# Splitting q, k and v on ScalarE and VectorE instead of GpSimd, and pacing attention by phase

## Chip, core and metric

One core of a Trainium2 chip runs the program. The metric is its time on the device in microseconds (us), the median of several runs of the same program.

## What is computed

Attention with a sigmoid in place of the softmax, over 8 batches of 12 heads, 448 positions and 64 values a head, feeds an MLP with a piecewise activation. In the reference (cut):

```
scores = scale * np.matmul(q, k.transpose(0, 1, 3, 2)) - np.log(S)     # scale = 1/8, S = 448
attn = 1.0 / (1.0 + np.exp(-scores))
x = np.matmul(attn, v)            # then (8*448, 768): 12 heads side by side
h = x @ w_in                      # w_in 768 x 2048
g = np.where(h >= 1, h, np.where(h <= -1, 0.0, (h + 1) ** 2 / 4))
out = g @ w_out                   # w_out 2048 x 768
```

## The kernel before

All large products run in 16 bit. To keep more digits, a 32-bit operand is scaled and **split**: a high part, the value rounded to 16 bit, and a low part, the remainder; a product of two split operands is three products, high by high, high by low and low by high.

*Attention.* The unit is a pair p of heads, six pairs a batch, 48 in all. Pairs 0 to 7 are used in full 32 bit, pairs 8 to 13 have q and k split, and pairs from 14 on have q, k and v split. `prep_a` (L323) finds the sums of the absolute values of a pair, `prep_b` (L344) turns them into scales, on VectorE, and splits (L365 to L375). Up to pair 16 the split is one ScalarE instruction for the high part (L368) and one VectorE instruction for the low part (L369), for each of q, k and v. From pair 17 (QA = 17) GpSimd does it with three instructions for each: scale in place (L373), round (L374), subtract (L375). A pair goes through four pieces of 128, 128, 128 and 64 keys. `scores` (L410) forms a piece's scores in PSUM (L438), `weigh` (L462) takes the sigmoid on ScalarE (L474) and splits it, high part on ScalarE (L482), low part on VectorE (L483), and `av` (L490) multiplies by v (L520). The last piece of a pair uses a block-diagonal copy of k's last 64 positions, the **corner**, two copies a pair (L454; on VectorE for pairs under CORN = 10, otherwise on GpSimd, and only pairs from 14 on have one).

*MLP.* For batches 0 and 1 the first products (L748, `up`) run plainly over 16 chunks of 128 hidden units. Beside batch 1's products the first weights are mixed (`mix`, L648, on VectorE and ScalarE; buffers pass through DMAs to HBM and back) for a scheme with seven block products instead of eight. From batch 2 on `up_blocks` (L699) does seven products of nine matmuls for each of eight block pairs; VectorE and ScalarE add the quarters up (L723, L726, L732) and `bend` (L755) applies the activation, five instructions for each of 16 chunks: L761 and L764 on ScalarE, L762, L763 and L765 on VectorE. `down` (L769) then does the second products, 288 matmuls a batch (L784). At the end of a batch `start_blocks` and `finish_blocks` (L549, L555) find the maximum of the next x through a product with a diagonal matrix (L163, L173), take four differences of blocks of x (L563 to L566, two on GpSimd by TP = 1) and split seven blocks of x (L569, L570).

*Order.* While batch b is multiplied, attention of batch b + 1 is worked in between, 24 steps a batch. The list `units` of product units is walked, and a table `share` (L933) says how many of the 24 steps are due by each unit: every unit counts DW = 8, but in batch 1 the first 24 units count 4, half. From batch 2 on there are 56 units of first products and 48 of second ones, with all steps due by unit 92. On top of that a scheduler arranges each engine's instructions by priority and its own estimates, so a change in one place can reorder an engine's whole queue. Each engine then works its queue strictly in turn, and waits where an operand is not there.

Of the kernel before, what the change touches and what calls it, by code (L numbers as in the profile page):

```python
# [19 lines left out]
ALU = mybir.AluOpType  # L20
# [30 lines left out]
LSTEP = 3  # L51

SB = 2
QA = 17
QT = 3
CORN = 10
GROUPED = 14
RUN_PRIO = 600
TP = 1

DW = 8
MIX0 = 24
# [9 lines left out]
def sigmoid_attention_mlp(ctx: ExitStack, tc: tile.TileContext, first_qvk, qkv, w_in, w_out, out_t):  # L72
# [271 lines left out]
    def prep_b(p):  # L344
        if not NFULL <= p < NPAIR or not first_time("split", p):
            return
        r, m = raws.pop(p), maxes.pop(p)
        n = 2 if p < NFULL + NHALF else 3
        m = sums.pop(p) if p in sums else all_sum(m, n)

        s, inv = scales(m, n, "qkv")
        sqk = sml_p.tile([P, 2], F32, tag="sqk", name="sqk")
        if n == 3:
            nc.vector.tensor_scalar(out=sqk[:, 1:2], in0=inv[:, 2:3], scalar1=1.0 / ATT, scalar2=None, op0=ALU.mult)
        nc.vector.tensor_scalar(
            out=sqk[:, 0:1], in0=inv[:, 0:1], scalar1=inv[:, 1:2], scalar2=1.0 / math.sqrt(D), op0=ALU.mult, op1=ALU.mult
        )
        hl = hls.pop(p, None) or stk_p.tile([P, 2, 2, S], F16, tag="hl", name="hl")
        parts = [hl[:, 0], hl[:, 1]]
        if n == 3:  # L360
            v = stk_p.tile([P, 2, VW], F16, tag="v", name="v", bufs=3)
            parts.append(v)
        else:
            v = ready[p]
        for t, dst in enumerate(parts):  # L365
            rt, hi = r[:, t * S : 2 * S + VW if t == 2 else (t + 1) * S], dst[:, 0, :]
            if p < QA and t != QT:
                nc.scalar.activation(hi, rt, AF.Copy, scale=s[:, t : t + 1])  # L368
                nc.vector.scalar_tensor_tensor(  # L369
                    out=dst[:, 1, :], in0=rt, scalar=s[:, t : t + 1], in1=hi, op0=ALU.mult, op1=ALU.subtract  # L370
                )
                continue
            nc.gpsimd.tensor_scalar(out=rt, in0=rt, scalar1=s[:, t : t + 1], scalar2=1.0, op0=ALU.mult, op1=ALU.mult)  # L373
            nc.gpsimd.tensor_scalar(out=hi, in0=rt, scalar1=1.0, scalar2=1.0, op0=ALU.mult, op1=ALU.mult)  # L374
            nc.gpsimd.tensor_tensor(out=dst[:, 1, :], in0=rt, in1=hi, op=ALU.subtract)  # L375

        ready[p] = hl, v, sqk

    pieces = {}
# [30 lines left out]
    def scores(todo):  # L410
# [37 lines left out]
        for p, c in (divmod(i, NPC) for i in todo):  # L448
            if c == 0 and p >= NFULL + NHALF:
                if p < NFULL + NHALF + 2:  # L450
                    nc.gpsimd.memset(corner(p), 0.0)
                for j in range(2):
                    rows = slice(j * D, (j + 1) * D)
                    (nc.vector if p < CORN else nc.gpsimd).tensor_copy(  # L454
                        out=corner(p)[rows, :, rows], in_=ready[p][0][rows, 1, :, NKC * P :]
                    )

# [97 lines left out]
    def finish_blocks(xm1, diag):  # L555
# [5 lines left out]
        b11, b12, b21, b22 = (x4[:, r, :, j, :] for r in range(2) for j in range(2))  # L561
        t1, t2, t3, t4 = (rows[:, k * HC * HN : (k + 1) * HC * HN].rearrange("p (c n) -> p c n", c=HC) for k in range(4))
        nc.vector.tensor_tensor(out=t1, in0=b12, in1=b11, op=ALU.subtract)  # L563
        (nc.gpsimd if TP else nc.vector).tensor_tensor(out=t3, in0=b22, in1=b12, op=ALU.subtract)
        nc.vector.tensor_tensor(out=t2, in0=b22, in1=t1, op=ALU.subtract)
        (nc.gpsimd if TP else nc.vector).tensor_tensor(out=t4, in0=b21, in1=t2, op=ALU.subtract)  # L566
        for t, src in ((0, b11), (4, t2), (5, t3), (3, t1), (1, b21), (6, t4), (2, b22)):
            hi = xc[:, t, :, 0, :]
            nc.scalar.activation(hi, src, AF.Copy, scale=s)  # L569
# [354 lines left out]
    for b in range(1, B):  # L924
# [5 lines left out]
            last = len(units) - LAST1  # L930
        first = at

        share = [DW // 2 if b < SB and u < NA * NCC // 2 else DW for u in range(last)]  # L933
        share = [sum(share[:u]) / sum(share) for u in range(last + 1)]
        with ExitStack() as order:
            if b >= PM:
# [63 lines left out]
```

## Time and profile before

| | |
|---|---|
| timed runs, median (lowest to highest) | 1156.87 us (1155.78 to 1158.25) |
| the profiled execution, its own time | 1152.84 us |
| its span, first to last instruction | 1151.1 us |
| TensorE (PE) busy | 1120.0 us, 97% |
| VectorE (DVE) busy | 831.4 us, 72% |
| ScalarE (ACT) busy | 721.2 us, 63% |
| GpSimd (POOL) busy | 291.3 us, 25% |
| mean granted TensorE clock | 0.998 of full |

The profile is one execution on the chip. The matrix engine is PE, and PEld its loading of weights, which runs beside it. An engine's busy time over the whole span says little here, since the stages differ; the same numbers by stretch, the list of what TensorE waited for, and the instructions just ahead of a wait say more. A row of grouped instructions ends with the idle time just before them and what ended it.

### The profile page before, as it was taken

The numbers are of one execution on the slowest core, as the hardware profiler recorded it, in microseconds if no ns is written. First come the engines' busy times: TensorE is split into PE (matmuls) and PEld (weight loads), VectorE is DVE, ScalarE is ACT, GpSimd is POOL, SyncE is SP. The second block draws the span as 40 slices with busy tenths as digits, with TensorE's granted clock in tenths as the row PEclk, the third lists the DMA queues.
The fourth block names the chain that finished last, engine by engine and source line by source line (L and its number), as shares of the span: only waits on it lengthen the run. The fifth ranks groups of instructions, "written<-read, shape, count | busy, mean of one in ns | idle before, by whom it ended". The sixth has DMA issues, their size and how long they took to land.

```text
span 1151.1 us, 20032 instructions
## 1 busy us (share of the span) xinstructions
PE 1120.0 (97%) x7914; PEld 660.7 (57%) x7914; DVE 831.4 (72%) x1730; ACT 721.2 (63%) x1199; POOL 291.3 (25%) x367
## 2 busy tenths in 40 slices
PE   8899999999889999999999999999999998999998
PEld 2234434444446775478645776457754677548954
DVE  6988977789985996469945798368974599646820
ACT  6978988679765785457754687347773476423410
POOL 0000000003442344323623353515344234110000
PEclk9999999999999999999999999999999999999999
DMA  9933432153453653125421345114532054103300
GB/s 367 394 107 132 162 124 74 35 192 119 161 182 120 220 193 108 49 91 193 157 105 50 130 170 195 50 50 169 186 140 69 22 189 173 65 17 123 136 24 25
DMA packets 32511, 151.64 MB, mean 132 GB/s; under 512 B 3488, under 2 KB 14240, under 8 KB 26272
## 3 DMA queue, kind: packets, MB, share of 16 engines
q1 hardware_dynamic: 30688, 140.92, 33.8%
q10 hardware_dynamic: 1728, 9.44, 2.2%
q8 instruction: 62, 1.02, 0.4%
q14 instruction: 33, 0.27, 0.1%
HBM read 126.94 MB, written 23.40 MB: 131 GB/s over the span
## 4 chain that ended last, share of the span: by engine, by line
PE 67%; DVE 20%; ACT 7%; issue 2%; DMA 2%; SPq 0%; DVEq 0%; ACTq 0%
PE po L784 35%; PE ph L714 11%; PE ph L748 8%; PE pav L520 6%; DVE ahl L483 5%; PE psc L438 4%; DVE g L762 4%; DVE g L763 3%; DVE xhl L723 2%; ACT ahl L482 2%; ACT psc L474 2%; DVE ghl L765 1%; PE psc L429 1%; DMA blocks<-mixs 1%; ACT ghl L764 1%
## 5 line engine op out<-in xcount | busy, mean ns | idle before, releaser
L784 PE MATMUL po<-ghl,w_out_sb 128*128 128x448 f16 x2304 | 447.7, 354 | 2.9 <-DVE g L763 2.9
L784 PEld LDWEIGHTS <-w_out_sb 128*128 128x128 f16 x2304 | 222.5, 98 | 220.4 <-issue 19.5
L714 PE MATMUL ph<-w_in_sb 128*128 128x224 f16 x3024 | 303.7, 259 | 10.6 <-DVE xhl L723 10.5
L714 PEld LDWEIGHTS <-w_in_sb 128*128 128x128 f16 x3024 | 284.4, 98 | 37.7 <-issue 36.4
L483 DVE SCALAR_TENSOR_TENSOR ahl<-psc,ahl 128x896 f16<-128x896 f32 (+1 forms) x170 | 153.0, 900 | 113.2 <-ACT ahl L482 111.4
L474 ACT ACTIVATE psc<-psc,nls,sqk 128x896 f32<-128x896 f32 (+1 forms) x136 | 130.3, 971 | 116.6 <-PE psc L438 113.4
L373 POOL TENSOR_SCALAR raw<-raw,qkv_s 128x448 f32<-128x448 f32 (+1 forms) x93 | 68.6, 752 | 427.6 <-DVE qkv_i L137 368.5
L482 ACT ACTIVATE ahl<-psc 128x896 f16<-128x896 f32 (+1 forms) x170 | 128.0, 762 | 23.3 <-DVE ahl L483 21.8
L748 PE MATMUL ph<-xhl,w_in_sb 128*128 128x448 f16 x576 | 112.8, 353 | 0.0
L761 ACT ACTIVATE g<-xhl,hr,ihr 128x448 f32<-128x448 f32 x96 | 67.8, 753 | 56.4 <-DVE xhl L723 56.2
L764 ACT ACTIVATE ghl<-g 128x448 f16<-128x448 f32 x128 | 73.2, 572 | 46.5 <-DVE g L763 46.4
L765 DVE TENSOR_TENSOR ghl<-g,ghl 128x448 f16<-128x448 f32 x128 | 91.1, 718 | 11.9 <-ACT ghl L764 11.0
L723 DVE TENSOR_TENSOR xhl<-ph,xhl 128x224 f32<-128x224 f32 x240 | 86.3, 382 | 16.9 <-PE ph L714 10.6
L762 DVE SCALAR_TENSOR_TENSOR g<-g,rk 128x448 f32<-128x448 f32 x112 | 83.9, 764 | 14.8 <-ACT g L761 14.3
L438 PE MATMUL psc<-hl 64*128 64x448 f16 x756 | 91.3, 352 | 0.3 <-ACT a L471 0.3
L748 PEld LDWEIGHTS <-w_in_sb 128*128 128x128 f16 x576 | 54.6, 98 | 59.9 <-issue 9.7
L520 PE MATMUL pav<-ahl,v 128*64 128x448 f16 x748 | 83.7, 357 | 0.0
L375 POOL TENSOR_TENSOR hl<-raw,hl 128x448 f16<-128x448 f32 x62 | 72.5, 1190 | 0.0
L797 DVE TENSOR_SCALAR o<-po,od 128x448 f32<-128x448 f32 x42 | 28.5, 679 | 59.0 <-PE po L784 58.8
L763 DVE SCALAR_TENSOR_TENSOR g<-xhl,ihs,g 128x448 f32<-128x448 f32 x96 | 69.3, 739 | 0.1
L337 ACT ACTIVATE dump<-raw 128x448 f16<-128x448 f32 (+1 forms) x105 | 61.5, 586 | 2.7 <-DVE mb L154 1.3
L454 POOL COPY w_in_sb<-hl 64x128 f16<-64x128 f16 x68 | 27.8, 409 | 129.3 <-DVE hl L369 127.4
(149 smaller groups left out, 1080.0 us busy)
## 6 DMA issues: line engine op xcount, KB each, us to landing
w_in_sb<-blocks SPq DMA_DIRECT2D x48, 1344.0 KB, 6.0
raw<-qkv SPq DMA_DIRECT2D x34, 704.0 KB, 4.2
w_out_sb<-w_in SPq DMA_DIRECT2D x16, 768.0 KB, 11.1
out_t<-o SPq DMA_DIRECT2D x48, 224.0 KB, 1.9
blocks<-mixs SPq DMA_DIRECT2D x8, 768.0 KB, 3.3
w_out_sb<-w_out ACTq DMA_DIRECT2D x6, 768.0 KB, 4.9
raww<-w_out ACTq DMA_DIRECT2D x6, 768.0 KB, 5.3
blocks<-mixp SPq DMA_DIRECT2D x8, 576.0 KB, 3.4
```

The lines of the kernel that those rows point to most:

```text
L438: run(lambda: nc.tensor.matmul(out, hl[rows, 1, kh, w], hl[rows, 0, qh, :], start=t == 0, stop=t == 2))
L474: nc.scalar.activation(a, a, AF.Sigmoid, bias=nls, scale=sqk)
L482: nc.scalar.activation(hi, x, AF.Copy, scale=ATT)
L483: made.setdefault(i, []).append(nc.vector.scalar_tensor_tensor(out=lo, in0=x, scalar=ATT, in1=hi, op0=ALU.mult, op1=ALU.subtract))
L520: run(lambda: once(nc.tensor.matmul(pav[j * D : (j + 1) * D, :S], *terms[j][t], start=c == 0 and t == 0, stop=mid and t == len(terms[j]) - ...
L714: nc.tensor.matmul(out, w[:, wt, wh, c * P : (c + 1) * P], xc[:, xt, c, xh, :], start=j in (0, 2) and c + wh + xh == 0, stop=c == HC - 1 a ...
L723: add = lambda out, q, other: nc.vector.tensor_tensor(out=out, in0=quarter(q), in1=other, op=ALU.add)
L748: nc.tensor.matmul(ph[:, :S], w_in_sb[:, f, wh, c * P : (c + 1) * P], xhl[:, c, xh, :], start=c == 0 and wh + xh == 0, stop=c == NCC - 1 a ...
L762: nc.vector.scalar_tensor_tensor(out=g, in0=g, scalar=rt, in1=g, op0=ALU.min, op1=ALU.mult)
L763: nc.vector.scalar_tensor_tensor(out=g, in0=h, scalar=ihs, in1=g, op0=ALU.mult, op1=ALU.max)
L765: (nc.gpsimd if f % GPOOL else nc.vector).tensor_tensor(out=ghl[:, f, 1, :], in0=g, in1=hi, op=ALU.subtract)
L784: nc.tensor.matmul(po[:, :S], w_out_sb[:, f, wh, m * P : (m + 1) * P], ghl[:, f, gh, :], start=f == lo and wh + gh == 0, stop=f == hi - 1 ...
```

## The change

The split of every pair is done by ScalarE and VectorE, in the form that pairs up to 16 have before; all corner copies are done by VectorE; all four differences of x are done by VectorE; and the table `share` counts half for the units of all first products, in batch 1 (both halves of them) and in the later batches. GpSimd is left with work at the start alone. No product is added or taken away.

```diff
--- before.py
+++ after.py
@@ -51,12 +51,8 @@
 LSTEP = 3
 
 SB = 2
-QA = 17
-QT = 3
-CORN = 10
 GROUPED = 14
 RUN_PRIO = 600
-TP = 1
 
 DW = 8
 MIX0 = 24
@@ -364,16 +360,10 @@
             v = ready[p]
         for t, dst in enumerate(parts):
             rt, hi = r[:, t * S : 2 * S + VW if t == 2 else (t + 1) * S], dst[:, 0, :]
-            if p < QA and t != QT:
-                nc.scalar.activation(hi, rt, AF.Copy, scale=s[:, t : t + 1])
-                nc.vector.scalar_tensor_tensor(
-                    out=dst[:, 1, :], in0=rt, scalar=s[:, t : t + 1], in1=hi, op0=ALU.mult, op1=ALU.subtract
-                )
-                continue
-            nc.gpsimd.tensor_scalar(out=rt, in0=rt, scalar1=s[:, t : t + 1], scalar2=1.0, op0=ALU.mult, op1=ALU.mult)
-            nc.gpsimd.tensor_scalar(out=hi, in0=rt, scalar1=1.0, scalar2=1.0, op0=ALU.mult, op1=ALU.mult)
-            nc.gpsimd.tensor_tensor(out=dst[:, 1, :], in0=rt, in1=hi, op=ALU.subtract)
-
+            nc.scalar.activation(hi, rt, AF.Copy, scale=s[:, t : t + 1])
+            nc.vector.scalar_tensor_tensor(
+                out=dst[:, 1, :], in0=rt, scalar=s[:, t : t + 1], in1=hi, op0=ALU.mult, op1=ALU.subtract
+            )
         ready[p] = hl, v, sqk
 
     pieces = {}
@@ -451,7 +441,7 @@
                     nc.gpsimd.memset(corner(p), 0.0)
                 for j in range(2):
                     rows = slice(j * D, (j + 1) * D)
-                    (nc.vector if p < CORN else nc.gpsimd).tensor_copy(
+                    nc.vector.tensor_copy(
                         out=corner(p)[rows, :, rows], in_=ready[p][0][rows, 1, :, NKC * P :]
                     )
 
@@ -561,9 +551,9 @@
         b11, b12, b21, b22 = (x4[:, r, :, j, :] for r in range(2) for j in range(2))
         t1, t2, t3, t4 = (rows[:, k * HC * HN : (k + 1) * HC * HN].rearrange("p (c n) -> p c n", c=HC) for k in range(4))
         nc.vector.tensor_tensor(out=t1, in0=b12, in1=b11, op=ALU.subtract)
-        (nc.gpsimd if TP else nc.vector).tensor_tensor(out=t3, in0=b22, in1=b12, op=ALU.subtract)
+        nc.vector.tensor_tensor(out=t3, in0=b22, in1=b12, op=ALU.subtract)
         nc.vector.tensor_tensor(out=t2, in0=b22, in1=t1, op=ALU.subtract)
-        (nc.gpsimd if TP else nc.vector).tensor_tensor(out=t4, in0=b21, in1=t2, op=ALU.subtract)
+        nc.vector.tensor_tensor(out=t4, in0=b21, in1=t2, op=ALU.subtract)
         for t, src in ((0, b11), (4, t2), (5, t3), (3, t1), (1, b21), (6, t4), (2, b22)):
             hi = xc[:, t, :, 0, :]
             nc.scalar.activation(hi, src, AF.Copy, scale=s)
@@ -930,7 +920,9 @@
             last = len(units) - LAST1
         first = at
 
-        share = [DW // 2 if b < SB and u < NA * NCC // 2 else DW for u in range(last)]
+        n = NA * NCC // 2
+        slow = [*range(n), *range(2 * n, 3 * n)] if b < SB else range(len(PRODUCTS) * NFC // 2)
+        share = [DW // 2 if u in slow else DW for u in range(last)]
         share = [sum(share[:u]) / sum(share) for u in range(last + 1)]
         with ExitStack() as order:
             if b >= PM:
```

In the later batches the 56 units of first products now count 4 each and the 36 units after them 8 each, so 10.5 of the 24 steps are due by the end of the first products, where it was 14.6.

The first place where the order moves that matters here is VectorE's queue in the first products of a later batch, where the scales of a batch's third pair are formed (L133 and L137 form the scales of q, k and v and their inverses; L723 is an addition; L762 and L763 are steps of the activation; L530 is a reduction of x). Before:

```order
L133 TENSOR_SCALAR qkv_s<-qkv_e 128x3
L137 TENSOR_SCALAR qkv_i<-qkv_e 128x3
L723 TENSOR_TENSOR xhl<-ph,xhl 128x224 x3
L354 TENSOR_SCALAR sqk<-qkv_i 128x1
L355 TENSOR_SCALAR sqk<-qkv_i 128x1
L762 SCALAR_TENSOR_TENSOR g<-g,rk_3327 128x448
L762 SCALAR_TENSOR_TENSOR g<-g,rk_3317 128x448
L763 SCALAR_TENSOR_TENSOR g<-xhl,ihs_3331,g 128x448
L723 TENSOR_TENSOR xhl<-ph,xhl 128x224
L763 SCALAR_TENSOR_TENSOR g<-xhl,ihs_3321,g 128x448
L530 TENSOR_REDUCE xm<-x_92 128x1
L723 TENSOR_TENSOR xhl<-ph,xhl 128x224
```

In the changed kernel line numbers are lower by 4 to 10. L133 forms the inverses, L364 is the low part of a split, L444 a corner copy, L713 an addition, L473 the low part of the weights and L752 a step of the activation:

```order
L133 TENSOR_SCALAR qkv_i<-qkv_e 128x3
L350 TENSOR_SCALAR sqk<-qkv_i 128x1
L351 TENSOR_SCALAR sqk<-qkv_i 128x1
L364 SCALAR_TENSOR_TENSOR hl<-raw,qkv_s,hl 128x448
L713 TENSOR_TENSOR xhl<-ph,xhl 128x224 x2
L364 SCALAR_TENSOR_TENSOR hl<-raw,qkv_s,hl 128x448
L364 SCALAR_TENSOR_TENSOR v<-raw,qkv_s,v 128x512
L713 TENSOR_TENSOR xhl<-ph,xhl 128x224
L444 COPY w_in_sb<-hl 64x2x64
L473 SCALAR_TENSOR_TENSOR ahl<-psc,ahl 128x896
L444 COPY w_in_sb<-hl 64x2x64
L752 SCALAR_TENSOR_TENSOR g<-g,rk_3318 128x448
```

The three splits and two corner copies of a pair have come between the scales and the activation steps, with the additions among them.

The second place is VectorE's queue at the end of batch 1, up to the diagonal that TensorE's maximum needs (L654 to L661 and L668 are mixing). Before:

```order
L654 TENSOR_TENSOR mixa<-w_in_sb 128x768 x2
L530 TENSOR_REDUCE xm<-x_92 128x1
L565 TENSOR_TENSOR xhl<-x_92,xhl 128x672
L797 TENSOR_SCALAR o<-po,od 128x448
L658 TENSOR_TENSOR mixa<-mixa 128x384
L552 TENSOR_REDUCE xm_3253<-xm 128x1
L483 SCALAR_TENSOR_TENSOR ahl<-psc,ahl 128x896 x2
L659 SCALAR_TENSOR_TENSOR mixa<-mixa,mixes 128x384
L163 TENSOR_SCALAR diag<-ident,xm_3253 128x128
```

In the changed kernel, with the three splits of a pair just ahead of these rows (L554 to L556 are differences of x, L649, L650 and L658 mixing, L159 the diagonal):

```order
L444 COPY w_in_sb<-hl 64x2x64 x2
L473 SCALAR_TENSOR_TENSOR ahl<-psc,ahl 128x896
L520 TENSOR_REDUCE xm<-x_92 128x1
L554 TENSOR_TENSOR xhl<-x_92 128x672
L555 TENSOR_TENSOR xhl<-x_92,xhl 128x672
L649 SCALAR_TENSOR_TENSOR mixa<-mixa,mixes 128x384
L473 SCALAR_TENSOR_TENSOR ahl<-psc,ahl 128x896
L542 TENSOR_REDUCE xm_3244<-xm 128x1
L556 TENSOR_TENSOR xhl<-x_92,xhl 128x672
L650 SCALAR_TENSOR_TENSOR mixa<-mixa,mixes 128x384
L658 SCALAR_TENSOR_TENSOR mixs<-mixa,mixes,mixs 128x2x384
L159 TENSOR_SCALAR diag<-ident,xm_3244 128x128
```

A pair's splits and copies and two differences more now stand ahead of the diagonal, and more of the last mixing step.

## Rows read from the trace of the kernel before

**Rows 1.** Windows: stretch, length, then busy us (instructions) of PE, PEld, DVE, ACT, POOL.
```profile
252.00:342.00 90.00, 83.87 (x491) 39.41 (x490) 78.85 (x128) 68.73 (x109) 34.25 (x37) 0.98 0.44 154
...
499.75:636.43 136.68, 134.66 (x1058) 87.56 (x1059) 98.16 (x213) 86.54 (x152) 53.59 (x68) 1.00 0.34 124
...
909.76:1043.79 134.03, 130.87 (x1024) 86.00 (x1024) 96.04 (x196) 72.40 (x115) 39.31 (x46) 1.00 0.27 97
...
499.75:571.70 71.95, 69.93 (x673) 55.82 (x674) 63.89 (x129) 55.87 (x100) 33.92 (x42) 1.00 0.46 165
```

**Rows 2.** Waits of PE, 252 to 342 and 499.75 to 636.43: total, times, longest.
```profile
PE psc L173 <- DVE diag L163: 3.2, 1, 3.2
PE po L784 <- DVE g L763: 2.9, 1, 2.9
...
PE ph L714 <- DVE xhl L723: 1.7, 1, 1.7
```

**Rows 3.** Timeline before the wait in batch 3: start us, us, engine, line, operands, count.
```profile
547.40 1.63 DVE L762 SCALAR_TENSOR_TENSOR g<-g,rk 128x448 f32<-128x448 f32 x2 [0.35 <-ACT g L761]
...
551.71 1.88 PE L714 MATMUL ph<-w_in_sb 128*128 128x224 f16 x18 [1.68 <-DVE xhl L723]
```

**Rows 4.** Lines, 499.75 to 636.43, then the two of 1043.79 on: busy, mean ns.
```profile
L483 DVE SCALAR_TENSOR_TENSOR ahl<-psc,ahl 128x896 f16<-128x896 f32 (+1 forms) x30 | 27.0, 901 | 22.7 <-ACT ahl L482 22.4
...
L762 DVE SCALAR_TENSOR_TENSOR g<-g,rk 128x448 f32<-128x448 f32 x16 | 12.7, 813 | 1.5 <-ACT g L761 1.5
L765 DVE TENSOR_TENSOR ghl<-g,ghl 128x448 f16<-128x448 f32 x16 | 12.6, 791 | 1.2 <-ACT ghl L764 1.1
...
L563 DVE TENSOR_TENSOR xhl<-x 128x672 f32<-128x672 f32 x1 | 0.8, 845 | 0.0
...
L454 POOL COPY w_in_sb<-hl 64x128 f16<-64x128 f16 x12 | 4.5, 379 | 0.3
...
L762 DVE SCALAR_TENSOR_TENSOR g<-g,rk 128x448 f32<-128x448 f32 x16 | 10.7, 680 | 2.2 <-ACT g L761 2.2
...
L765 DVE TENSOR_TENSOR ghl<-g,ghl 128x448 f16<-128x448 f32 x16 | 9.7, 619 | 0.1
```

**Rows 5.** Lines of the whole run, shapes apart: early pairs' splits, a cast, a diagonal.
```profile
L368 ACT ACTIVATE hl<-raw,qkv_s 128x448 f16<-128x448 f32 x18 | 11.0, 664 | 0.6 <-DVE qkv_i L137 0.6
...
L368 ACT ACTIVATE v<-raw,qkv_s 128x512 f16<-128x512 f32 x3 | 2.1, 707 | 0.0
...
L369 DVE SCALAR_TENSOR_TENSOR hl<-raw,qkv_s,hl 128x448 f16<-128x448 f32 x18 | 11.7, 678 | 0.5 <-ACT hl L368 0.5
...
L369 DVE SCALAR_TENSOR_TENSOR v<-raw,qkv_s,v 128x512 f16<-128x512 f32 x3 | 2.2, 746 | 0.0
...
L154 DVE CAST mb<-m 128x2 bf16<-128x2 f32 x6 | 1.0, 166 | 5.2 <-ACT dump L337 5.2
...
L163 DVE TENSOR_SCALAR diag<-ident,wi_x 128x128 bf16<-128x128 bf16 x2 | 0.5, 250 | 0.0
```

**Rows 6.** Timeline of PE in batch 3: first products, scores, weighted sums, second products.
```profile
499.68 6.21 PE L714 MATMUL ph<-w_in_sb 128*128 128x224 f16 x63
505.82 1.31 PE L438 MATMUL psc<-hl 64*128 64x448 f16 x12
507.06 1.14 PE L520 MATMUL pav<-ahl,v 128*64 128x448 f16 x10
...
577.24 9.25 PE L784 MATMUL po<-ghl,w_out_sb 128*128 128x448 f16 x48
```

**Rows 7.** DVE in batch 1: lines of 252 to 342, then the timeline there.
```profile
L654 DVE TENSOR_TENSOR mixa<-w_in_sb 128x768 f32<-128x768 f16 x12 | 13.8, 1193 | 8.6 <-DMA blocks<-mixs 8.6
...
318.88 1.83 DVE L654 TENSOR_TENSOR mixa<-w_in_sb 128x768 f32<-128x768 f16 x2 [3.05 <-DMA blocks<-mixs]
...
331.76 2.91 DVE L654 TENSOR_TENSOR mixa<-w_in_sb 128x768 f32<-128x768 f16 x2 [3.06 <-DMA blocks<-mixs]
...
340.23 1.59 DVE L163 TENSOR_SCALAR diag<-ident,xm 128x128 bf16<-128x128 bf16 x1
```

## Prediction

> **What bounds the kernel now.** I read the table by stretch first. From 363 us on the program repeats: batches 2 to 5 are each a stretch of some 136.7 us of which TensorE is busy 134.66, and batch 6 is nearly so [rows 1]. VectorE has 98.16 us of work there and ScalarE 86.54, so over a whole batch neither is the limit; TensorE is, and all a change can win is TensorE's idle time. The list of waits says where that lies [rows 2]: in each of batches 2 to 5, 1.7 us behind the additions of L723, of 2.0 in all (136.68 less 134.66 [rows 1]); 3.2 us in batch 6 (134.03 less 130.87 [rows 1]); and in 252 to 342 us, where batch 1's products run and the weight blocks are mixed, 6.1 us (90.00 less 83.87 [rows 1]), 2.9 of it behind L763 and 3.2 behind the diagonal of L163. That is 6.1 + 4 x 2.0 + 3.2 = 17.3 us. Each of the named waits is on VectorE. Within a batch VectorE is full only during the first products: 63.89 us busy of the 71.95 from 499.75 to 571.70 [rows 1].
>
> The timeline of the wait itself shows why [rows 3]. Some 4 us ahead of the addition that TensorE gets at 551.71, two L762 took 1.63 us, more than twice 0.68, while GpSimd was splitting a pair. In the last batch, where GpSimd does nothing, L762 takes 680 ns and L765 619, against 813 and 791 in batch 3 [rows 4]. So GpSimd's work stretches VectorE's: 16 x (0.813 - 0.680) = 2.1 us and 16 x (0.791 - 0.619) = 2.8 us per batch, 4.9 together, nearly all during the first products.
>
> The Trainium skill (SBUF — State Buffer, Who interferes with whom) says that a VectorE instruction with two SBUF inputs and a GpSimd instruction that reads SBUF exclude each other for a whole instruction. Taken alone it would price the relief higher: GpSimd is busy 53.59 us of 136.68, so some 19 of 48 such instructions would meet one, and at half of its mean instruction, 53.59 / 68 = 0.79 us, that is an estimated 7.5 us; VectorE would then gain 2.6 us more per batch. The rows say 4.9, and I use them.
>
> **The change part by part.** *Splits of pairs 17 to 47.* GpSimd loses nine instructions a pair. ScalarE gets two of 664 ns and one of 707, VectorE two of 678 and one of 746 [rows 5]: 2.0 and 2.1 us a pair, 12.2 and 12.6 a batch. *Corner copies.* Twelve a batch go from GpSimd, 379 ns each [rows 4], to VectorE. No row shows VectorE copying 64x128; above, I bound it by GpSimd's 0.38, below by the 0.17 of a VectorE cast of two columns [rows 5]; I take 0.25, nearer to the lower, whose engine it is: 3.0 us a batch (2.0 to 4.5). *Differences of x.* Two more on VectorE at L563's 845 ns [rows 4], 1.7 us a batch; the next one then has no GpSimd beside it. VectorE's total per batch: 98.2 + 12.6 + 3.0 + 1.7 - 4.9 = 110.6 us, ScalarE's 86.5 + 12.2 = 98.7. Both stay under TensorE's 134.7, so only places matter.
>
> *Where the attention goes.* Half rate in the first products moves attention into the second ones. Counted in the order between the first and the last addition of a batch, VectorE loses four L483 (11 + 7 become 9 + 5), one reduction and a set of scales, and gains nine splits and six corner copies. An instruction's row holds about 0.08 us that overlaps the next. The four L483 at a mean of 901 ns [rows 4] are 3.3 us, the rest about 1.1: 4.4 off. Nine splits are 5.6 us and six copies about 1.2: 6.8 on. The relief takes off some 4.5. VectorE's work in the stretch falls by about 2 us. TensorE's falls by more: 12 score products at 0.103, 10 of the weighted sums at 0.11 and 14 second products at 0.193 [rows 6] leave it, 1.2 + 1.1 + 2.7 = 5.0 us. **So VectorE is 3 us tighter against TensorE in that stretch than before**, from about 62 against 67 us to about 60 against 62. What still speaks for a gain is how the lateness arises: by bursts. TensorE may start a further block when the two last additions of the one before the last are done; in between it has 18 products of 0.0975 us [rows 6], 1.76 us, less 0.6 for the two additions: about 1.2 us of lateness is free. Before, contention put up to 3 us into one block (the one at 545 to 553). Laid out block by block, with the after order's VectorE work against its TensorE work, VectorE is late by up to about 2 us in the fourth block and again in the seventh (9.2 us of its work against 7.8), where a split waits for ScalarE as well (I allow 0.4 us a pair). Past the free 1.2 us that is 0.9 and 0.6 us of waiting. I take 1.5 us a batch in place of 2.0 (0 to 4), and 2.7 in place of 3.2 for batch 6: -2.0 and -0.5 us.
>
> *Queues that it moves past.* In VectorE's queue the additions and the bends now stand behind splits; in ScalarE's, sigmoids stand behind the split's three copies. GpSimd's queue is empty, so nothing waits there; SP's loads of raw pairs waited for GpSimd's last subtraction and are now free earlier. The maximum of x (one product that needs the diagonal) stands behind 49 second products instead of 54, and covers the split of x with 56 instead of 66, 10.8 us against 12.7 at 0.193 [rows 6]. The list has no wait there now [rows 2], and the first product needs only the first of seven parts of x, so I cost it at nothing; if the cover proves too short, the cost is at most the 1.9 us lost, per batch.
>
> *Batch 1, 252 to 342 us.* Three pairs' splits (6.3 us), four pairs' corner copies (2) and two differences (1.7) come onto VectorE, 10 us; and what GpSimd stretched there goes: twelve L654 took 1.193 us each where a free pair of them takes 1.83, 3.3 us over; the diagonal took 1.59 against 0.25 [rows 5, 7], 1.3 over; eight bends at batch 3's excess are 2.5, and the other steps of mixing I put at 1 to 3: some 9 us. So VectorE's path from the ninth block of products to the diagonal stays about as long as it was. But TensorE gets there later without waiting: counted in its order it has 80.0 us of work from there to the maximum, where it had 75.4 plus the first wait of 2.9, since 73 second products instead of 97 are left behind the maximum. The first wait goes too, because L763 comes some 4 us sooner. I take 1.5 us of waiting in place of 6.1 (0 to 6): **-4.6 us.** The loads of weight blocks between mixing steps (3.06 us before the last two L654 [rows 7]) stay as they are.
>
> *Changeovers.* TensorE's order has 67 runs a batch instead of 64; what its slots leave unexplained of 134.7 us is about 1.3, 0.02 each: +0.3 in all.
>
> **Sum.** -4.6 - 2.0 - 0.5 + 0.3 = -6.8 us against the profiled execution, 1152.84 to 1146.0. The profiled one lies 4.0 below the median of the timed runs, 1156.87, so 1150.
>
> **The rivals.** *All waits go.* If the bursts were only GpSimd's doing, the 17.3 us go whole: 1139.5. For it: every stretched row stands beside a GpSimd row. Against: VectorE remains 97% full in the first products.
>
> *VectorE stops behind ScalarE (slower).* A VectorE split can't begin before ScalarE's copy, and ScalarE serves its queue in turn; with a sigmoid of 1.0 us ahead, VectorE stands idle some 1.5 us a pair instead of 0.4, three times in a stretch that has 2 us to spare: 3.3 us more, 4.8 a batch, 2.8 above before. Five batches give +14, batch 1 gives back 4.6: 1166. It decides from about 0.9 us a pair on. Against: the 18 splits of early pairs waited 0.5 us in all for ScalarE. The Trainium skill (Perfetto Trace Analysis, Optimizing Scalar/DVE Operations) advises to offload to ScalarE or even GpSimd where VectorE is saturated, with the reservation that GpSimd shares its port; the change goes the other way in the one stretch that is nearly saturated, and this rival is that advice coming true.
>
> *Waits only move.* In batch 1 the splits and differences ahead of the diagonal take what GpSimd's absence gives, and batches 2 to 6 keep their 2 us: -2 to 0, so 1155.
>
> **How the numbers follow.** Forecast (1143 to 1153) 0.50; all waits gone 0.15; only moved 0.15; slower 0.20. About 0.2%, 2.3 us, is what a measurement here can tell from no change. Faster is 0.50 + 0.15, same 0.15, slower 0.20. The range takes in most of the first rival and the near half of the second, 1140 to 1163; what is left out is the far slow end and a little below the floor.
>
> **What would show it.** Right: no GpSimd work after the start; L762 and L763 at 0.68 and L765 at 0.62 us in batch 3; VectorE near 110 us a batch; TensorE waiting 1 to 2 us a batch on L723's additions and under 2 us before batch 2. Wrong: more than 3 us a batch of TensorE idle, with VectorE idle behind ScalarE's split just before; or a wait for the diagonal of over 4 us in batch 1; or waits of TensorE in the second products, which this has at nothing.

## The result, and the profile after

| | before | after |
|---|---|---|
| timed runs beside each other, median (lowest to highest) | 1157.56 us (1155.78 to 1160.34) | 1142.64 us (1142.4 to 1143.43) |
| profiled execution, own time | 1152.84 us | 1142.46 us |
| its span | 1151.1 us | 1140.7 us |
| VectorE and ScalarE busy, batch 3 | 98.16, 86.54 us | 105.87, 96.86 us |

The ratio is 0.9879, 95% interval 0.9857 to 0.99. The change is faster, by 14.9 us (1.2%) between the medians and 10.4 between the profiled executions; 1150 was forecast, with 1140 to 1163 as range. The 4.5 us between these two differences go at least in part with the clock that TensorE was granted, as the part on the prediction shows.

Cut at TensorE's first product of batch 2, of batch 6 and of the last batch, the two spans divide so:

| stretch | before | after | difference |
|---|---|---|---|
| start to batch 2 | 363.00 | 360.34 | -2.7 |
| batches 2 to 5 | 546.69 | 541.79 | -4.9 |
| batch 6 | 133.94 | 130.86 | -3.1 |
| last batch, end | 107.47 | 107.71 | +0.2 |

The windows of after (stretch, length, then busy us of PE, PEld, DVE, ACT, POOL) answer to [rows 1]: batch 1's stretch, the first products of batch 3 up to their last addition, batch 3, batch 6.

```profile
252.00:342.00 90.00, 86.77 (x497) 41.47 (x496) 79.69 (x141) 70.84 (x111) 0.00 (x0) 0.98 0.44 159
495.79:563.52 67.73, 67.03 (x652) 55.01 (x651) 61.96 (x136) 54.70 (x101) 0.00 (x0) 1.00 0.50 181
495.79:631.23 135.44, 134.74 (x1060) 87.37 (x1058) 105.87 (x245) 96.86 (x170) 0.00 (x0) 1.00 0.34 125
902.13:1032.99 130.86, 130.56 (x1023) 86.21 (x1022) 97.27 (x219) 80.26 (x133) 0.00 (x0) 1.00 0.28 100
```

TensorE is idle 0.70 us in batch 3 (135.44 less 134.74) where it was 2.0, 0.3 in batch 6 where it was 3.2, and 3.2 in batch 1's stretch where it was 6.1. Its waits of the whole run (total, times, longest) answer to [rows 2]; those at the start of the program are left out. L713 is L723 of before, L753 is L763:

```profile
PE ph L704 <- DVE xhl L713: 3.5, 5, 0.7
...
PE po L774 <- DVE g L753: 2.0, 1, 2.0
PE ph L738 <- DVE g L753: 0.9, 1, 0.9
PE pav L510 <- DVE ahl L473: 0.4, 1, 0.4
```

The wait for the diagonal has gone. The one on the additions is 0.7 us in each of batches 2 to 5 and in the last batch, where before has 0.7 us as well; batch 6 has none. The waits on L753 in batch 1 add up to the 2.9 us that stood there before. VectorE's lines in batch 3 (busy, mean ns, idle before) answer to [rows 4, 5]:

```profile
L752 DVE SCALAR_TENSOR_TENSOR g<-g,rk 128x448 f32<-128x448 f32 x16 | 10.6, 680 | 0.6 <-ACT g L751 0.5
L753 DVE SCALAR_TENSOR_TENSOR g<-xhl,ihs,g 128x448 f32<-128x448 f32 x16 | 10.5, 679 | 0.0
L755 DVE TENSOR_TENSOR ghl<-g,ghl 128x448 f16<-128x448 f32 x16 | 9.8, 621 | 1.1 <-ACT ghl L754 0.9
L364 DVE SCALAR_TENSOR_TENSOR hl<-raw,qkv_s,hl 128x448 f16<-128x448 f32 x12 | 7.8, 682 | 1.4 <-ACT hl L363 1.4
...
L364 DVE SCALAR_TENSOR_TENSOR v<-raw,qkv_s,v 128x512 f16<-128x512 f32 x6 | 4.5, 748 | 0.0
...
L444 DVE COPY w_in_sb<-hl 64x128 f16<-64x128 f16 x12 | 2.2, 186 | 0.1
...
L150 DVE CAST mb<-m 128x3 bf16<-128x3 f32 x6 | 1.0, 167 | 5.6 <-PE psc L153 5.6
...
L555 DVE TENSOR_TENSOR xhl<-x,xhl 128x672 f32<-128x672 f32 x1 | 0.9, 851 | 0.0
```

The activation steps take the time that the last batch of before had; a split is as long as it was for the early pairs; a corner copy takes 186 ns.

### The profile page after: what moved, and what is told of

The parts are those of the page before. It is cut to its first block, busy times and chain, and to the rows that moved or that the text cites. A ratio compares the mean times of both kernels' runs of the same rounds, so it can differ in the third digit from the quotient of the medians.

```text
span 1140.7 us, 19832 instructions
## 1 busy us (share of the span) xinstructions
PE 1121.1 (98%) x7914; PEld 660.4 (58%) x7914; DVE 865.1 (76%) x1903; ACT 773.0 (68%) x1292; POOL 1.6 (0%) x8
## 4 chain that ended last, share of the span: by engine, by line
PE 77%; DVE 10%; ACT 7%; DMA 5%; issue 1%; SPq 1%; DVEq 0%; ACTq 0%
PE po L774 37%; PE ph L704 17%; PE ph L738 8%; PE pav L510 8%; PE psc L428 6%; DMA w_out_sb<-w_in 2%; DVE ahl L473 1%; PE psc L419 1%; DVE g L753 1%; DVE g L752 1%; DVE xhl L713 1%; ACT dump L333 1%; ACT psc L464 1%; DVE ghl L755 1%; DMA raw<-qkv 1%
## 5 line engine op out<-in xcount | busy, mean ns | idle before, releaser
L774 PEld LDWEIGHTS <-w_out_sb 128*128 128x128 f16 x2304 | 220.0, 98 | 224.7 <-issue 28.4
L473 DVE SCALAR_TENSOR_TENSOR ahl<-psc,ahl 128x896 f16<-128x896 f32 (+1 forms) x170 | 153.0, 901 | 73.4 <-ACT ahl L472 71.5
L472 ACT ACTIVATE ahl<-psc 128x896 f16<-128x896 f32 (+1 forms) x170 | 127.6, 761 | 22.1 <-DVE ahl L473 20.6
L713 DVE TENSOR_TENSOR xhl<-ph,xhl 128x224 f32<-128x224 f32 x240 | 87.1, 385 | 25.1 <-PE ph L704 21.5
L755 DVE TENSOR_TENSOR ghl<-g,ghl 128x448 f16<-128x448 f32 x128 | 78.6, 620 | 10.1 <-ACT ghl L754 9.0
L752 DVE SCALAR_TENSOR_TENSOR g<-g,rk 128x448 f32<-128x448 f32 x112 | 74.6, 680 | 7.5 <-ACT g L751 7.0
L333 ACT ACTIVATE dump<-raw 128x448 f16<-128x448 f32 (+1 forms) x105 | 61.3, 585 | 9.8 <-DMA raw<-qkv 7.9
L363 ACT ACTIVATE hl<-raw,qkv_s 128x448 f16<-128x448 f32 x80 | 48.9, 658 | 26.4 <-DVE qkv_s L129 25.4
L753 DVE SCALAR_TENSOR_TENSOR g<-xhl,ihs,g 128x448 f32<-128x448 f32 x96 | 63.2, 679 | 0.1
L510 PEld LDWEIGHTS <-v 128*64 128x64 f16 x748 | 36.5, 109 | 37.8 <-issue 17.8
L428 PEld LDWEIGHTS <-hl 64*128 64x128 f16 x756 | 27.8, 94 | 50.6 <-issue 27.9
```

The lines of the kernel that those rows point to most:

```text
L428: run(lambda: nc.tensor.matmul(out, hl[rows, 1, kh, w], hl[rows, 0, qh, :], start=t == 0, stop=t == 2))
L472: nc.scalar.activation(hi, x, AF.Copy, scale=ATT)
L473: made.setdefault(i, []).append(nc.vector.scalar_tensor_tensor(out=lo, in0=x, scalar=ATT, in1=hi, op0=ALU.mult, op1=ALU.subtract))
L510: run(lambda: once(nc.tensor.matmul(pav[j * D : (j + 1) * D, :S], *terms[j][t], start=c == 0 and t == 0, stop=mid and t == len(terms[j]) - ...
L713: add = lambda out, q, other: nc.vector.tensor_tensor(out=out, in0=quarter(q), in1=other, op=ALU.add)
L752: nc.vector.scalar_tensor_tensor(out=g, in0=g, scalar=rt, in1=g, op0=ALU.min, op1=ALU.mult)
```

## Experiments

**Theory:** GpSimd's work stretches VectorE's in the first products, and moving it gains; attention moved out of the first products lets TensorE run without waits there; each helps the other. **Rivals:** the pacing alone does it (R1), or the move alone does it and pacing adds nothing or costs (R2). The runs of before beside the experiments lay between 1152.17 and 1161.37 us, with medians of 1154.84, 1155.72 and 1156.4 in the three sets.

### The two parts apart

*Pacing alone:* the kernel before with the new table.

```diff
-        share = [DW // 2 if b < SB and u < NA * NCC // 2 else DW for u in range(last)]
+        n = NA * NCC // 2
+        slow = [*range(n), *range(2 * n, 3 * n)] if b < SB else range(len(PRODUCTS) * NFC // 2)
+        share = [DW // 2 if u in slow else DW for u in range(last)]
```

> The kernel before with the new table of shares alone; GpSimd still splits, copies corners and takes differences. Theory (both parts are needed: the rate makes room on VectorE in the first products, the move takes GpSimd's stretching away): TensorE's waits fall from 2.0 to about 1 us in batches 2 to 5 and from 6.1 to about 4 in batch 1, L762 stays near 0.81 us: some 6 us below before, 1151. Rival R1 (the rate alone did it): as the changed kernel, 1143. Rival R2 (the move alone did it): 1157.

Measured: 1153.76 us (1153.23 to 1155.4), ratio 0.999 (0.998 to 0.9999). Batch 3 takes 136.87 us (TensorE busy 135.06), batch 2 begins 2.9 us later than in before, batch 6 is 2.5 shorter. Its waits of TensorE in batch 3:

```profile
PE ph L714 <- DVE xhl L723: 0.9, 1, 0.9
PE psc L438 <- DVE qkv_e L129: 0.8, 1, 0.8
```

The wait on the additions is halved, and another, of scores for the sum that VectorE reads, takes its place. R1 is out. The theory's 1151, with about 1 us of waiting a batch, is missed too: 1.8 us are left (136.87 less 135.06).

*The move alone:* the changed kernel with the old table (the diff above, reversed).

> The changed kernel with the old table of shares; everything is on ScalarE and VectorE. Theory (both): VectorE's first products hold four more low parts and as much splitting as they can take, 65 us against TensorE's 67, without GpSimd's bursts: waits of 1 to 2 us a batch, 3 to 5 in batch 1: about 1152. R1 (rate alone): 1157 or slower, since VectorE has more work and no relief in rate. R2 (move alone): 1143, L762 at 0.68 us and waits under 1 us a batch.

Measured: 1146.21 us (1145.77 to 1147.85), ratio 0.9922 (0.9901 to 0.9942). So the move is the larger part, 8.6 us, and the pacing adds 3.6 on top (the changed kernel's median is from another set of runs), where alone it was worth 1.1. Between the profiled executions, which share out the 10.4 us, the move is worth 6.7 and the pacing on top of it 3.7, where pacing alone lost 1.5. But in batches 2 to 5 the move alone hardly shortens the waiting: batch 3 takes 136.07 us of which TensorE is busy 134.27, so 1.8 us of idle remain. VectorE's timeline shows what replaced the stretched steps ahead of it (start us, us):

```profile
544.32 1.27 DVE L364 SCALAR_TENSOR_TENSOR hl<-raw,qkv_s,hl 128x448 f16<-128x448 f32 x2
545.51 0.74 DVE L364 SCALAR_TENSOR_TENSOR v<-raw,qkv_s,v 128x512 f16<-128x512 f32 x1
546.17 0.38 DVE L444 COPY w_in_sb<-hl 64x128 f16<-64x128 f16 x2
...
548.68 0.38 DVE L713 TENSOR_TENSOR xhl<-ph,xhl 128x224 f32<-128x224 f32 x1
...
549.12 4.47 PE L704 MATMUL ph<-w_in_sb 128*128 128x224 f16 x45 [1.80 <-DVE xhl L713]
```

A pair's splits and copies, 2.3 us in one piece, stand ahead of the addition. R2 has the larger part right, but not that pacing adds nothing, nor waits under 1 us a batch; the theory had the waits right and the time, 1152, too high by 6 us.

*Splits moved and pacing, but corner copies and differences left on GpSimd:* the kernel before with the new table and

```diff
-QA = 17
+QA = 48
```

> The changed kernel except that GpSimd keeps the corner copies and the two differences of x. Theory: these are small and stand where TensorE does not wait, so within 2 us of the changed kernel, 1142 to 1145. Rival (corners and differences matter, as GpSimd's differences lengthen VectorE's own and its diagonal): 1147 or more, with the wait for the diagonal of batch 1 back at 2 us or more.

Measured: 1143.55 us (1143.13 to 1144.61), ratio 0.9896 (0.988 to 0.9913); a batch takes 135.46 us, as after. By these runs copies and differences are worth some 0.9 us, within the theory's range. The rival's sign is there all the same: TensorE waits 2.1 us for the diagonal of batch 1, and 5.5 us on VectorE around it (240 to 361 us) where the changed kernel waits 3.3. The mean granted clock was higher here, 1.0 against 0.997 in the profiled executions, so 0.9 may be too little. The splits are the larger part.

### GpSimd beside VectorE

*First try:* the changed kernel, and after each pair's split GpSimd repeats its nine old steps in place on the raw buffer, with results that nothing uses.

```diff
         ready[p] = hl, v, sqk
+        if p >= 17:
+            parts = [r[:, t * S : 2 * S + VW if t == 2 else (t + 1) * S] for t in range(3)]
+            for t, rt in enumerate(parts):
+                w = rt.shape[1]
+                lo = parts[t == 0].bitcast(F16)[:, :w]
+                nc.gpsimd.tensor_scalar(out=rt, in0=rt, scalar1=s[:, t : t + 1], scalar2=1.0, op0=ALU.mult, op1=ALU.mult)
+                nc.gpsimd.tensor_scalar(out=lo, in0=rt, scalar1=1.0, scalar2=1.0, op0=ALU.mult, op1=ALU.mult)
+                nc.gpsimd.tensor_tensor(out=lo, in0=rt, in1=lo, op=ALU.subtract)
```

> The changed kernel, with GpSimd doing the nine instructions of before on each pair's raw buffer after the split, for nothing: its results are not used. All else, TensorE's order too, is nearly the changed kernel's. Theory (GpSimd's work stretches VectorE's and TensorE waits for that): L752 and L755 (before's L762 and L765) back at 0.78 to 0.82 us, VectorE 4 to 6 us a batch longer, TensorE's waits 2 to 4 us a batch instead of 0.7: about 1152 (1147 to 1158). Rival (the stretching is real but covered, the gain is pacing and order): 1142 to 1145.

Measured: 1176.2 us (1174.84 to 1178.59), ratio 1.018 (1.0158 to 1.0201), far above either expectation. It can't be read as stretch alone: the raw buffers are now held until GpSimd is done, and ScalarE's sums (L333) waited 20.0 us for loads into them:

```profile
ACT dump L333 <- DMA raw<-qkv: 20.0, 4, 5.1
```

*Without that:* the same steps on a small buffer of GpSimd's own, half as wide and twice as many.

```diff
         ready[p] = hl, v, sqk
+        for t in range(6 if p >= 17 else 0):
+            sc = s[:, t // 2 : t // 2 + 1]
+            nc.gpsimd.tensor_scalar(out=spin, in0=spin, scalar1=sc, scalar2=1.0, op0=ALU.mult, op1=ALU.mult)
+            nc.gpsimd.tensor_scalar(out=spin16, in0=spin, scalar1=1.0, scalar2=1.0, op0=ALU.mult, op1=ALU.mult)
+            nc.gpsimd.tensor_tensor(out=spin16, in0=spin, in1=spin16, op=ALU.subtract)
```

> The changed kernel, and GpSimd once more works beside it: after each split of pairs 17 to 47 it runs the three kinds of step that it had in the kernel before (scale, round, subtract) on a small buffer of its own, with results that nothing uses. TensorE's, VectorE's and ScalarE's queues keep the order of the changed kernel, and no buffer is held longer. If GpSimd's mere presence beside VectorE cost time (theory: the two-input steps L762 and L765 of before, here L760 and L763, go back from 680 and 620 ns to about 800 and 790 on average, most of it in the first products), VectorE gains some 5 us of work a batch, TensorE waits 2 to 4 us a batch in place of 0.7, and the time is 1150 to 1160 us. Rival: the gain came from a split that is done sooner and in VectorE's own order, and the stretch is absorbed; then 1142 to 1145 us with TensorE's waits as in the changed kernel.

Measured: 1160.38 us (1159.54 to 1161.61), ratio to before 1.0039 (1.0024 to 1.0054): 17.7 us above the changed kernel, just past the upper end of the theory, and above before. TensorE, VectorE and ScalarE run the same instructions in the same order as in the changed kernel, each in its queue, from first to last. Batch 3's window:

```profile
503.43:640.85 137.42, 135.33 (x1060) 87.50 (x1058) 114.74 (x245) 97.01 (x170) 63.48 (x108) 1.00 0.34 123
```

Four of VectorE's lines in it, two steps of the activation (here L760 and L763), splits (here L367) and corner copies (here L452):

```profile
L760 DVE SCALAR_TENSOR_TENSOR g<-g,rk 128x448 f32<-128x448 f32 x16 | 11.4, 730 | 0.6 <-ACT g L759 0.5
L763 DVE TENSOR_TENSOR ghl<-g,ghl 128x448 f16<-128x448 f32 x16 | 10.5, 662 | 1.1 <-ACT ghl L762 0.9
L367 DVE SCALAR_TENSOR_TENSOR hl<-raw,qkv_s,hl 128x448 f16<-128x448 f32 x12 | 10.2, 886 | 1.4 <-ACT hl L366 1.4
...
L452 DVE COPY w_in_sb<-hl 64x128 f16<-64x128 f16 x12 | 3.6, 296 | 0.1
```

And TensorE's waits there:

```profile
PE psc L427 <- DVE ahl L481: 1.2, 1, 1.2
PE ph L712 <- DVE xhl L721: 0.9, 4, 0.4
```

No instruction was added to VectorE, and its busy time grew from 105.87 to 114.74 us; the same splits take 886 ns instead of 682, the copies 296 instead of 186. TensorE waits 2.1 us in place of 0.7. The steps of the activation, which the theory expected back at some 800 and 790 ns, took 730 and 662; over half of the growth is in splits and copies. GpSimd is busier here (63.48 us) than in before (53.59 [rows 1]), and it works right behind each split, so 17.7 us is not the price in before; that its mere presence costs this much is shown.

### Other paces

In the table of the changed kernel the units of first products of batches 2 to 6 count 4. With 3, 5 and 6:

```diff
-        share = [DW // 2 if u in slow else DW for u in range(last)]
+        share = [(DW // 2 if b < SB else 3) if u in slow else DW for u in range(last)]
```

> The changed kernel with the units of first products of batches 2 to 6 counted 3 instead of 4 (8.8 of the 24 steps of attention due by their end instead of 10.5). If VectorE's bursts in the first products are still what TensorE waits for, the 0.7 us a batch shrink to 0 to 0.4 and the time is 1140 to 1142 us. Rival: the second products are now the fuller ones for VectorE, waits on the scores or weighted sums appear there, and the time is 1143 to 1147 us.

Measured with 3: 1140.13 us (1138.57 to 1140.86), ratio 0.9863 (0.9837 to 0.9888), as expected of a VectorE that has room: no wait of TensorE on the additions is left in batches 2 to 5.

> The changed kernel with those units counted 5 instead of 4 (12 of 24 steps due by their end). The waits on the additions grow from 0.7 to about 1 us a batch: 1143 to 1145 us. Rival: the order around the bursts decides and not the rate: anything from 1141 to 1147 us without a trend over 3, 4, 5 and 8.

Measured with 5: 1139.62 us (1139.1 to 1140.77), ratio 0.9861 (0.9836 to 0.9886). More attention in the first products than after has, and less time: the expectation's theory is wrong, and the time lies below the rival's range as well.

> The changed kernel with 6 instead of 4 in batches 2 to 6. Periods of a batch so far by the number counted: 3 gives 134.9, 4 gives 135.45, 5 gives 134.7, 8 gives 136.1 us. If crowding of VectorE in the first products sets the waits, 6 lies between 5 and 8, at 134.9 to 135.8 and 1140 to 1144 us. If it is chance of the order alone, it may lie anywhere from 134.7 to 136.5, 1139.5 to 1148 us.

Measured with 6: 1145.89 us (1145.55 to 1146.76), ratio 0.9908 (0.9889 to 0.9928). A batch takes 135.63 us, which crowding allowed, but the time is past its 1144 and inside the range of an order by chance. And the kernel before, GpSimd's splits and all, with 5 in batches 2 to 6 and batch 1 as it was:

```diff
-        share = [DW // 2 if b < SB and u < NA * NCC // 2 else DW for u in range(last)]
+        late = len(PRODUCTS) * NFC // 2
+        share = [DW // 2 if b < SB and u < NA * NCC // 2 else 5 if b >= SB and u < late else DW for u in range(last)]
```

> The kernel before, GpSimd's splits and all, with 5 instead of 8 for the units of first products in batches 2 to 6; batch 1 is paced as before. With 4 (and batch 1 paced at half as well) nothing was gained. If GpSimd's stretching of VectorE takes the gain whatever the rate, a batch stays at 136.3 to 137 us and the time at 1151 to 1155. If 4 was only an unlucky order, a batch falls to 135 to 136 us and the time to 1144 to 1150 us.

Measured: 1153.95 us (1152.05 to 1156.25), ratio 0.9982 (0.9967 to 0.9997), as expected if GpSimd takes the gain at any rate. The profiled batch 3 of each kernel, its length and TensorE's idle time in it, us:

| units count | splits on GpSimd: length (idle) | splits on ScalarE and VectorE: length (idle) |
|---|---|---|
| 8 | 136.68 (2.02) | 136.07 (1.80) |
| 6 | | 135.63 (0.64) |
| 5 | 136.60 (2.07) | 134.69 (0.28) |
| 4 | 136.87 (1.81) | 135.44 (0.70) |
| 3 | | 134.93 (0.00) |

With GpSimd's splits some 2 us of waiting stay at every pace tried. Without them they stay at 8, and 0 to 0.7 us are left at 6, 5, 4 and 3. So in these batches neither part takes the wait away, and both together take most of it or all. What holds it in the left column shows in VectorE's and GpSimd's timeline of the kernel before at pace 5, ahead of its wait:

```profile
554.98 2.41 POOL L375 TENSOR_TENSOR hl<-raw,hl 128x448 f16<-128x448 f32 x2
555.48 1.02 DVE L762 SCALAR_TENSOR_TENSOR g<-g,rk 128x448 f32<-128x448 f32 x1
...
556.72 1.15 DVE L762 SCALAR_TENSOR_TENSOR g<-g,rk 128x448 f32<-128x448 f32 x1
557.35 1.53 POOL L375 TENSOR_TENSOR v<-raw,v 128x512 f16<-128x512 f32 x1
557.79 1.57 DVE L763 SCALAR_TENSOR_TENSOR g<-xhl,ihs,g 128x448 f32<-128x448 f32 x1
559.28 0.38 DVE L723 TENSOR_TENSOR xhl<-ph,xhl 128x224 f32<-128x224 f32 x1
...
559.72 2.94 PE L714 MATMUL ph<-w_in_sb 128*128 128x224 f16 x29 [1.59 <-DVE xhl L723]
```

Three activation steps of 0.68 us took 3.74. The right column isn't a smooth trend either. Part of it is TensorE's busy time, 134.27, 134.41, 134.74 and 134.93 us at 8, 5, 4 and 3, where its order has 60, 63, 67 and 71 unbroken stretches of one kind of product a batch. That each change of kind costs time would fit, some 0.06 us a change, but it is not shown: pace 6 has 66 and 134.99, and the kernel with GpSimd's idle work has 67 like the changed one and 135.33. Why 4 waits longer than 5 is open as well.

### Batch 1, and a better version

Batch 1's second half of first products at a quarter of the rate:

```diff
-        share = [DW // 2 if u in slow else DW for u in range(last)]
+        share = [2 if b < SB and 2 * n <= u < 3 * n else DW // 2 if u in slow else DW for u in range(last)]
```

> The changed kernel with batch 1's second half of first products at a quarter of the rate instead of half, and nothing else; batches 2 to 6 keep their order. There TensorE waits 2.9 us for L753, because VectorE is full from 270 to 292 us with mixing, a pair's split and the activation. Theory: with less attention there the two waits fall to 0 to 1 us: 1140 to 1142 us. Rival: mixing alone fills VectorE there and the attention comes back later beside the rest of the mixing: 1142 to 1146 us.

Measured: 1143.47 us (1142.52 to 1144.28), ratio 0.9893 (0.9872 to 0.9913); batch 2 begins at 362.36 instead of 360.34. The waits on L753 went (0.2 left), and scores and weighted sums wait 4.9 us ahead of batch 2 instead. The rival was right.

Pace 5 in batches 2 to 5 and 4 in batch 6:

```diff
-        share = [DW // 2 if u in slow else DW for u in range(last)]
+        share = [(DW // 2 if b < SB or b + 2 >= B else 5) if u in slow else DW for u in range(last)]
```

> The changed kernel with 5 instead of 4 for the units of first products in batches 2 to 5, and 4 as it was in batch 6. With 5 everywhere a batch took 134.7 us instead of 135.45, but batch 6 took 131.9 instead of 130.9. If a batch's time depends on its own order alone, both gains add up: 1138 to 1139.5 us. Rival: batch 6 starts from another state of the buffers and keeps 131.9: 1139.5 to 1140.5 us.

Measured: 1139.6 us (1138.63 to 1139.61), ratio 0.9851 (0.9831 to 0.987). Batch 3 takes 134.72, batch 6 130.88 us, as each did alone, so the batches add up as the theory has it. The time doesn't show it: 1139.6 is just inside the rival's range, and pace 5 in all batches had 1139.62. Last, the same with the mixing begun earlier:

```diff
-MIX0 = 24
+MIX0 = 18
```

> As the kernel above, and the mixing of the first weights in batch 1 begins at the 18th unit instead of the 24th. VectorE is full from 270 to 292 us, and TensorE waits there 2.9 to 3.5 us for L753. If a longer time for the mixing loosens that, 1136 to 1138 us. Rival: the eight mixing steps are held by their loads and stores to HBM, the full place only moves: 1138 to 1141 us.

Measured: 1139.21 us (1138.41 to 1141.46), ratio 0.9852 (0.9832 to 0.9873): the rival; batch 2 begins 0.4 us earlier, which the runs can't tell from nothing. Both lie some 3 us under the changed kernel; their slowest runs, 1139.61 and 1141.46, are under its fastest, 1142.4, though from another set of runs.

## Why the prediction was right in sign, and where its terms were off

The measured 1142.64 us lies inside the stated range but just below the forecast's own 1143 to 1153, 3.1 us above the rival "All waits go" and 7.4 below 1150. The mechanism held; the terms below were off, one of them the other way than the rest. Of its signs of being right, GpSimd's silence and the activation steps at 0.68 and 0.62 us came; VectorE near 110 us, 1 to 2 us of waiting a batch and under 2 us before batch 2 did not (105.87, 0.7 and 3.2).

*What bounds the kernel.* This held: TensorE's waits on VectorE, 17.3 us, are all that was won from. Of these, 3.2 + 4 x 0.7 + 0.3 = 6.3 are left, where 1.5 + 6.0 + 2.7 = 10.2 were forecast.

*VectorE's total.* Forecast 110.6 us a batch, measured 105.87. The splits were right (12.3 for 12.6). A copy at 186 ns makes 2.2 for 3.0. The relief was too small: it was summed over L762 and L765, and four more lines of before were stretched:

```profile
L763 DVE SCALAR_TENSOR_TENSOR g<-xhl,ihs,g 128x448 f32<-128x448 f32 x16 | 11.3, 719 | 0.0
...
L154 DVE CAST mb<-m 128x3 bf16<-128x3 f32 x6 | 1.9, 319 | 5.5 <-PE psc L157 5.5
L565 DVE TENSOR_TENSOR xhl<-x,xhl 128x672 f32<-128x672 f32 x1 | 1.4, 1424 | 0.0
...
L163 DVE TENSOR_SCALAR diag<-ident,xm 128x128 bf16<-128x128 bf16 x1 | 0.6, 634 | 0.0
```

Against after's means (L163 at the 250 ns of [rows 5]), they are 0.6, 0.9, 0.6 and 0.4 us; with 2.1 and 2.7 for L762 and L765 that makes 7.3 us, not 4.9. The differences cost the 1.7 us forecast. The remaining 1.2 us was not traced; the prediction puts the overlap of an instruction's row with the next at 0.08 us and leaves it out of this sum, and with 32 more instructions (213 to 245) that is an estimated 2.6 us. ScalarE came to 96.86 (98.7 forecast). Taking the two costliest rows for all was the mistake. The Trainium skill (SBUF — State Buffer, Who interferes with whom) had led to an estimate of 7.5 us for the relief; that the traces' 7.3 is near it is in part luck, since the estimate counted only the 48 activation steps, and these came to 2.1 + 0.6 + 2.7 = 5.4.

*The wait in batches 2 to 5* was the term that this mis-sized: 1.5 us forecast, 0.7 measured. "VectorE is 3 us tighter" was wrong in size: from a batch's first product to its last additions VectorE's work fell by 4.4 us, not 2 (66.4 in before's 74.5 us there, 61.96 now), TensorE's by 5.5 (72.5 to 67.03), so it is 1.0 us tighter; the row of after for this stretch stands with its windows, and before's is

```profile
499.68:574.20 74.52, 72.50 (x689) 57.20 (x688) 66.39 (x133) 55.94 (x100) 35.96 (x44) 1.00 0.44 160
```

The layout gave lateness in the fourth block and the seventh; only the one in the seventh came, 0.70 us against 0.6, and not for the reason given. No split waits for ScalarE there, the last one is done 15 us sooner; VectorE pauses for the high part of the weights (L472), and the activation follows:

```profile
538.68 1.09 DVE L473 SCALAR_TENSOR_TENSOR ahl<-psc,ahl 128x896 f16<-128x896 f32 x1 [0.72 <-ACT ahl L472]
...
543.80 0.38 DVE L713 TENSOR_TENSOR xhl<-ph,xhl 128x224 f32<-128x224 f32 x1
...
544.24 4.47 PE L704 MATMUL ph<-w_in_sb 128*128 128x224 f16 x45 [0.70 <-DVE xhl L713]
```

*Batch 6* was put at 2.7 us of waiting without a layout of its own, just a little under before. It has 0.3, and 3.1 us of the gain are there, 0.5 were forecast.

*Batch 1* was forecast too well: 1.5 us of waiting, measured 3.2. The diagonal's wait went, as laid out. "The first wait goes too, because L763 comes some 4 us sooner" failed. Of the relief counted for it, the 2.5 us of "eight bends at batch 3's excess" did not exist: in before the activation steps of this stretch, 252 to 342 us, took no longer than in the last batch, where GpSimd is idle:

```profile
L762 DVE SCALAR_TENSOR_TENSOR g<-g,rk 128x448 f32<-128x448 f32 x8 | 5.4, 681 | 1.7 <-ACT g L761 1.7
...
L765 DVE TENSOR_TENSOR ghl<-g,ghl 128x448 f16<-128x448 f32 x8 | 4.9, 614 | 0.0
```

And in the changed kernel VectorE has no pause for over 10 us before L753, with a pair's splits (L364) and mixing (L644) in the row:

```profile
283.65 1.27 DVE L364 SCALAR_TENSOR_TENSOR hl<-raw,qkv_s,hl 128x448 f16<-128x448 f32 x2
284.84 0.74 DVE L364 SCALAR_TENSOR_TENSOR v<-raw,qkv_s,v 128x512 f16<-128x512 f32 x1
...
287.45 1.82 DVE L644 TENSOR_TENSOR mixa<-w_in_sb 128x768 f32<-128x768 f16 x2
...
290.79 0.68 DVE L753 SCALAR_TENSOR_TENSOR g<-ph,ihs,g 128x448 f32<-128x448 f32 x1
...
291.52 6.38 PE L774 MATMUL po<-ghl,w_out_sb 128*128 128x448 f16 x24 [1.95 <-DVE g L753]
```

*From profile to median.* The sum came to 1146.0 for the profiled execution, measured 1142.46. Then 4.0 us were added because before's profiled run lies that far below its median; in the changed kernel the two differ by 0.2 us. That is the largest single miss, 3.8 of the 7.4 us between 1150 and 1142.64. The runs show what the distance goes with, the mean clock that TensorE was granted, as a share of full. Of the 45 runs of before beside the experiments the six at 0.999 took 1152.17 to 1154.1 us, the ten at 0.997 and 0.998 took 1152.39 to 1155.72, and the two at 0.991 took 1159.98 and 1161.37; 23 of the 45 had 0.995 or less. The profiled run had 0.998, and the changed kernel's four runs had 0.997 and 0.998. So the 10.4 us between the profiled executions, which the waits account for, say more of the change than the 14.9 between the medians. What lowers the clock in the runs of before is open.

*Changeovers:* three runs more a batch were priced at 0.06 us; TensorE's busy time grew by 0.08 (134.66 to 134.74), though that the changeovers cause it is not shown.

*The rivals.* "VectorE stops behind ScalarE" was to decide from 0.9 us a pair on; the row of L364 above has 1.4 us of idle before twelve splits of six pairs, 0.23 a pair, under the 0.4 allowed. "All waits go" is what the kernels at pace 3 and 5 show for batches 2 to 5, so the forecast's reason against it, VectorE's fullness in the first products, was not a floor. "Waits only move" is nearly what pacing alone did. The shorter cover of the second products cost nothing: no wait stands there in batches 2 to 6.

## What to carry to other kernels

Read what an engine's work costs its neighbours line by line over every row that reads the same memory, before counting what a move adds. Where waits come from bursts, look at how much work stands in one piece ahead of the late instruction and try a few paces, since two remedies can each do little alone. Don't carry the distance between a profiled run and the median from one kernel to its change; look at the granted clock of both first.

## What was not expected of the hardware

*Which VectorE instructions GpSimd stretches.* In before, over 360 to 1045 us, L765 took 0.62 us with no GpSimd instruction beside it and 1.21 to 1.57 beside a subtraction of L375; L483 and L723, which read one operand from PSUM, took 1.08 and 0.38 in either case, and so did the reduction of L530 with 0.61. A cast of three columns, 0.17 us alone, took 1.00 each of the four times it fell on L375:

```profile
431.97 3.07 POOL L375 TENSOR_TENSOR hl<-raw,hl 128x448 f16<-128x448 f32 x2
432.40 1.00 DVE L154 CAST mb<-m 128x3 bf16<-128x3 f32 x1
...
551.27 2.41 POOL L375 TENSOR_TENSOR hl<-raw,hl 128x448 f16<-128x448 f32 x2
...
551.58 1.21 DVE L765 TENSOR_TENSOR ghl<-g,ghl 128x448 f16<-128x448 f32 x1
552.71 1.08 DVE L483 SCALAR_TENSOR_TENSOR ahl<-psc,ahl 128x896 f16<-128x896 f32 x1
```

GpSimd pays as well: its L375 on 448 columns took 1.03 us at the least and 1.72 at the most. The Trainium skill (SBUF — State Buffer, Who interferes with whom) states that a VectorE instruction with at most one SBUF input, outside the modes that use both ports, doesn't contend with GpSimd, that one with two does when GpSimd's instruction reads SBUF, and that casts and copies can enter those modes. The rows agree in all three: L483, L723 and L530 for the first, L765 for the second, the cast above and the corner copies beside GpSimd's idle work (186 to 296 ns) for the third.

*Spread.* The kernel before spread over 9 us in the last set of 15 runs (1152.17 to 1161.37), the one at pace 5 with GpSimd's splits over 4; the changed kernel spread over 1.0 and the others with ScalarE's and VectorE's splits over 1.0 to 3.1. But the one with GpSimd's idle work beside them spread over only 2.1 in ten runs, and so did before with the new table, over 2.2 in ten, so GpSimd being busy is not enough for it. The spread goes with the granted clock, 0.991 to 0.999 in before and 0.997 to 1.0 in the kernels with ScalarE's and VectorE's splits alone; why the clock differs wasn't settled.
